# Batch 0 of a fused attention and feed-forward kernel: the first two head pairs' kv moved ahead of the second transposes

## The chip, the cores and the metric

The kernel runs on one core of one Trainium2 chip. A core has five engines that run their own instruction queues in order: TensorE (PE in the profile, its weight loads PEld), VectorE (DVE), ScalarE (ACT), GpSimd (POOL) and SyncE (SP), which here issues nearly all DMAs. TensorE writes to PSUM, which has eight banks; the other engines copy from there to SBUF. The metric is the time of one execution on the device in microseconds (us). Lower is better. The kernel before takes 256.82 us, the median of three runs (256.74 to 257.05).

## The reference

Inputs are q, k, v of shape 8 x 8 x 576 x 64 (batch, heads, sequence, head dimension) and two weights, `w_in` of 512 x 2048 and `w_out` of 2048 x 512. The first part is attention without a square matrix:

```python
q_s = exp(q - max(q, -1)); q_s = q_s / sum(q_s, -1)      # softmax over the head dimension
k_s = exp(k - max(k, 2));  k_s = k_s / sum(k_s, 2)       # softmax over the sequence
kv  = einsum('bhsd,bhse->bhde', k_s, v)
x   = einsum('bhsd,bhde->bhse', q_s, kv)                 # then heads side by side: 4608 x 512
```

The second part is a feed-forward layer on those 4608 rows: `h = x @ w_in`, `g = 0.5 * h * (1 + erf(h / sqrt(2)))`, `out = g @ w_out`.

## The kernel before, in words

The work goes batch by batch, 512 rows of each at a time (a ninth step does the 64 rows that are left of each batch). Every batch has the same stages: exp of q and k on ScalarE, sums and scaling of q on VectorE and GpSimd, transposes of the scaled q on TensorE, `kv`, then `x`, then `h` with its gelu, then `y`. From batch 1 on, the first three stages of a batch are done while TensorE is in the `h` and `y` of an earlier one. Batch 0 has nothing to hide behind: its stages stand at the start of the kernel, while q, k, v and the weights still arrive. `h` of batch 0 is the first of the long matmul stages.

The program is written with a manual schedule: on each engine the instructions stand in the order in which the Python code issues them, and semaphores make an engine wait where it needs another's result. So the order of the calls near the end of the kernel function is the order of the queues. For batch 0 the steps are these; a "half" is two of the four head pairs.

- `tp_mm(0, half)` (L287): eight 128x128 transposes of the scaled q into one PSUM bank. `tp_evac` copies the bank to `qT`; the first half is VectorE's (L296), the second ScalarE's (L298).
- `cast_v(0, hp, engine)`: v of one head pair, 128 x 576, from float32 to bfloat16 into `v_aug`. Pairs 0 and 1 are ScalarE's (L188), 2 and 3 are GpSimd's (L190). Each waits for the DMA of its pair.
- `kv_mm(0, half)` (L225): 36 matmuls on 64x64 quarters of the array, nine steps for each of two pairs and two heads. They need the exponentials of k and the two v pieces. A column of ones in `v_aug` gives the sums of k's softmax.
- `kv_norm(0, half)`: on VectorE, per pair a reciprocal (L236) and a scaling of `kv` into `kvc` (L238).
- `x_mm(0, half)` (L343): four matmuls of 512 columns on 64x64 quarters, from `kvc` and `qT`. `x_evac` copies each pair's result to its piece of `xT`, by ScalarE (L370) or VectorE (L368). `x_tile` only takes the PSUM bank.
- `cast_wi_dm` (L848, GpSimd) and `cast_wi` (L836 on GpSimd, L837 and L840 on VectorE): columns of `w_in` to bfloat16.
- `table(AF.Gelu)` (L100): ScalarE's function table is changed from exp to gelu.
- `h_phase(0, ...)` (L377, gelu L383): the first group makes two tiles of `h` at once: for piece 0 of `xT` one matmul each, then for piece 1, and so on; each matmul has 512 columns and needs that piece and the cast weights.

`psum_h`, `psum_y` and `psum_a` hand out banks in turn (banks 0 to 2, 3 and 4, and 5). Ahead of all this stand float32 matmuls on zeros (`warm`, L899), which keep TensorE busy while the first inputs land.

Of the kernel before, what the change touches and what calls it, by code (L numbers as in the profile page):

```python
# [16 lines left out]
def kernel(  # L17
# [16 lines left out]
    nc = tc.nc  # L34
    B, H, S, D = q.shape
# [6 lines left out]
    NDM = DM // 128  # L42
    NDF = DF // 128
    NS = S // 64
# [24 lines left out]
    psum_h, psum_y, psum_a = Banks(0, 1, 2), Banks(3, 4), Banks(5)  # L69
# [9 lines left out]
    v_aug = [singles.tile([128, HP, NS, VW], BF16, name=f"v_aug{i}") for i in range(2)]  # L79
# [22 lines left out]
    st = [dict() for _ in range(B + 1)]  # L102
# [78 lines left out]
                func=AF.Exp,  # L181
            )

    def cast_v(b, hp, eng=nc.vector):
        o = v_aug[b % 2][:, hp, :, 0:D]
        i = st[b]["vf"][:, hp, :].rearrange("p (n d) -> p n d", n=NS)
        if eng is nc.scalar:
            eng.copy(out=o, in_=i)  # L188
        else:
            eng.tensor_copy(out=o, in_=i)  # L190

    def cast_v_all(b):
        for hp in range(HP):
            cast_v(b, hp, nc.gpsimd)

    def kv_tiles(b, banks=(6, 7)):


        two = [bank(i, "kv", (128, 2, 256)) for i in banks]
        if b == 0:  # L200
            p = [psum_h.tile([128, 512], FP32, tag="h", name="kv")[:, 0:256] for i in range(2)]
            p += [ps[:, 0] for ps in two]
        else:
            st[b]["kvall"] = two
            p = [two[i // 2][:, i % 2] for i in place]
        st[b]["kv"] = p
# [3 lines left out]
    def kvc_of(b, hp):  # L210

        return kvc[b][:, hp if b < 2 else place[hp], :]

    def kv_mm(b, half):


        if "kv" not in st[b]:
            kv_tiles(b)
        for n in range(NS):
            for i in range(2):  # L220
                for hh in range(2):
                    hp = 2 * half + i
                    pr = slice(hh * 64, hh * 64 + 64)
                    c = slice((hh ^ i) * 64, (hh ^ i) * 64 + 64)
                    nc.tensor.matmul(  # L225
                        st[b]["kv"][hp][c, 0:D + 1], ek[b % 2][pr, hp, n, :],
                        v_aug[b % 2][pr, hp, n, 0:D + 1], start=(n == 0), stop=(n == NS - 1),
                    )

    def kv_norm(b, half=None):  # L230

        if half is not None:
            hps = (2 * half, 2 * half + 1)
            rec = small.tile([128, 2], FP32, tag="reck")
            for i, hp in enumerate(hps):
                nc.vector.reciprocal(rec[:, i:i + 1], st[b]["kv"][hp][:, D:D + 1])  # L236
            for i, hp in enumerate(hps):
                nc.vector.tensor_tensor(  # L238
                    out=kvc[b][:, hp, :], in0=st[b]["kv"][hp][:, 0:D],
                    in1=rec[:, i:i + 1].to_broadcast([128, D]), op=ALU.mult,  # L240
                )
            return
        for i, ps in enumerate(st[b]["kvall"]):
            rec = small.tile([128, 2], FP32, tag="reck")
            nc.vector.reciprocal(rec, ps[:, :, D])
            nc.vector.tensor_tensor(
                out=kvc[b][:, 2 * i:2 * i + 2], in0=ps[:, :, 0:D],
                in1=rec.unsqueeze(2).to_broadcast([128, 2, D]), op=ALU.mult,
            )
# [28 lines left out]
    def tp_mm(b, half):  # L278
        if half == 0:
            st[b]["qT"] = attn_sb.tile([128, J, HP, 128], BF16, tag="qT", name="qT", bufs=1)  # L280
        pool, tag = (psum_h, "h") if half == 1 else (psum_a, "a")
        ps = pool.tile([128, J, 2, 128], BF16, tag=tag)
        st[b][f"tp{half}"] = ps
        for i in range(2):
            hp = 2 * half + i
            for j in range(J):
                nc.tensor.transpose(  # L287
                    ps[:, j, i, :],
                    st[b]["eq"][:, j, 2 * hp:2 * hp + 2, :].rearrange("p h d -> p (h d)"),
                    identity,  # L290
                )

    def tp_evac(b, half, eng="v"):
        o = st[b]["qT"][:, :, 2 * half:2 * half + 2, :]
        if eng == "v":
            nc.vector.tensor_copy(out=o, in_=st[b][f"tp{half}"])  # L296
        else:
            nc.scalar.copy(out=o, in_=st[b][f"tp{half}"])  # L298
# [29 lines left out]
    def x_tile(b, hp, pool, tag):  # L328
        if "xT" not in st[b]:
            st[b]["xT"] = attn_sb.tile([128, HP, M], BF16, tag="xT", name="xT", bufs=1)  # L330
        st[b][f"x{hp}"] = pool.tile([128, M], FP32, tag=tag, name="ps")

    def x_mm(b, half):

        for bb in range(B if b == B else 1):
            for r in range(2):
                for i in range(2):
                    hp = 2 * half + i
                    pr = slice(r * 64, r * 64 + 64)
                    c = slice((r ^ i) * 64, (r ^ i) * 64 + 64)  # L340
                    ps = st[b][f"x{hp}"]
                    if b < B:
                        nc.tensor.matmul(  # L343
                            ps[c, :], kvc_of(b, hp)[pr], st[b]["qT"][pr, :, hp, :],
                            start=True, stop=True,
                        )
                    else:
                        nc.tensor.matmul(
                            ps[c, bb * R:(bb + 1) * R], kvc_of(bb, hp)[pr],
                            st[b]["qT"][pr, bb // 2, hp, bb % 2 * R:(bb % 2 + 1) * R],  # L350
                            start=(bb == 0), stop=True, skip_group_check=True,
                        )
# [12 lines left out]
    def x_evac(b, hp, eng="v"):  # L365
        ps = st[b][f"x{hp}"]
        if eng == "v":
            nc.vector.tensor_copy(out=st[b]["xT"][:, hp, :], in_=ps)  # L368
        else:
            nc.scalar.copy(out=st[b]["xT"][:, hp, :], in_=ps)  # L370
# [446 lines left out]
    def load_wi(i):  # L817

        w = wst.tile([128, NDM, 512], FP32, tag=f"w{i}", name="w")
        n = wi_cols[i]  # L820
        src = moe_w_in[:, wi_off[i]:wi_off[i] + n].rearrange("(c p) f -> p c f", p=128)
        d = NDM // wi_parts[i]
        for c in range(0, NDM, d):
            nc.sync.dma_start(out=w[:, c:c + d, 0:n], in_=src[:, c:c + d])
        return w
# [3 lines left out]
    def cast_wi(i, w, eng):  # L829
        n = wi_cols[i]  # L830
        r = n // 128
        o = wi_bf[:, :, wi_off[i]:wi_off[i] + n].rearrange("p d (c m) -> p d c m", c=r)
        w = w[:, :, 0:n].rearrange("p d (m c) -> p d c m", c=r)
        if eng == "pv":

            nc.gpsimd.tensor_copy(out=o[:, 0:2], in_=w[:, 0:2])  # L836
            nc.vector.tensor_copy(out=o[:, 2:4], in_=w[:, 2:4])  # L837
        else:
            for c in range(NDM):
                nc.vector.tensor_copy(out=o[:, c], in_=w[:, c])  # L840

    def cast_wi_dm(i, w, dm, eng):

        n = wi_cols[i]
        r = n // 128
        o = wi_bf[:, dm, wi_off[i]:wi_off[i] + n].rearrange("p (c m) -> p c m", c=r)
        w = w[:, dm, 0:n].rearrange("p (m c) -> p c m", c=r)
        eng.tensor_copy(out=o, in_=w)  # L848
# [63 lines left out]
    wi = [load_wi(i) for i in range(5)]  # L912
# [21 lines left out]
    norm_q(0, 1, 2, nc.vector)  # L934
    tp_mm(0, 0)
    cast_v(0, 0, nc.scalar)
    cast_v(0, 1, nc.scalar)
    tp_evac(0, 0)
    cast_v(0, 2, nc.gpsimd)
    cast_v(0, 3, nc.gpsimd)  # L940
    x_tile(0, 0, psum_y, "y")
    x_tile(0, 1, psum_y, "y")
    tp_mm(0, 1)
    tp_evac(0, 1, "s")
    x_tile(0, 2, psum_a, "a")
    kv_mm(0, 0)
    kv_norm(0, 0)
    kv_mm(0, 1)
    kv_norm(0, 1)
    for dm in range(NDM):  # L950
        cast_wi_dm(0, wi[0], dm, nc.gpsimd)
    x_tile(0, 3, psum_h, "h")
    x_mm(0, 0)
    x_evac(0, 0, "s")
    x_evac(0, 1)
    x_mm(0, 1)
    x_evac(0, 2, "s")
    x_evac(0, 3)
    cast_wi(1, wi[1], "pv")
    table(AF.Gelu)  # L960

# [190 lines left out]
```

## Time and profile before

| What | Value |
|---|---|
| median of 3 runs | 256.82 us |
| the profiled execution, time and span | 257.07 us, 255.3 us |
| TensorE busy | 248.8 us, 97% of the span |
| VectorE, ScalarE, GpSimd busy | 82%, 74%, 27% |
| first transposes start | 10.63 us |
| first `h` matmul of batch 0 starts | 14.35 us |
| `h` of batch 0, 64 matmuls | 14.35 to 28.34 us |
| mean granted clock of TensorE | 0.996 |

Times within the profile count from the start of the span. The profiled execution took 257.07 us in all, so 1.8 us lie around its span. A row of the timeline has a start, a length, the engine, the line of the kernel, the operation, what it writes and reads, how many instructions are merged, and in brackets how long the engine stood idle before it and what ended that. The matmul rows overlap, as matmuls are pipelined: the length of one is the time to its result, while the next starts much sooner.

### The profile page before, as it was taken

How to read it: one execution, taken by the hardware profiler on the slowest of the kernel's cores; microseconds unless marked ns; L12 is line 12 of the kernel's file. 1: busy time of each engine (PE TensorE's matmuls, PEld its weight loads, DVE VectorE, ACT ScalarE, POOL GpSimd, SP SyncE). 2: the span in 40 equal slices, each digit the busy share in tenths (PEclk: the TensorE clock that was granted, in tenths of full speed). 3: DMA queues.
4: the chain of work that ended last, by engine and by line, in shares of the span. 5: the costliest groups of instructions: out<-in, count | busy, mean ns of one | idle time of the engine just before them, and what ended most of it. 6: DMA issues, size and time to landing. Idle time of an engine off the chain costs nothing.

```text
span 255.3 us, 6533 instructions
## 1 busy us (share of the span) xinstructions
PE 248.8 (97%) x2678; PEld 196.1 (77%) x2678; DVE 208.1 (82%) x365; ACT 188.9 (74%) x320; POOL 67.8 (27%) x65
## 2 busy tenths in 40 slices
PE   7999999999999999999999999999999999999993
PEld 3444445448888888888888888888888888888882
DVE  1878796998986989897889788988898889488962
ACT  4875996699977995899589968896886787148720
POOL 1430034000735067006700580058001800040000
PEclk9999999999999999999999999999999999999998
DMA  7999999994449925980499059904920340022024
GB/s 236 396 389 424 403 406 399 400 410 166 62 143 335 265 65 126 328 336 1 114 299 369 7 95 314 374 3 86 270 63 3 82 164 3 0 87 82 1 54 113
DMA packets 43166, 50.23 MB, mean 197 GB/s; under 512 B 20224, under 2 KB 30464, under 8 KB 42880
## 3 DMA queue, kind: packets, MB, share of 16 engines
q1 hardware_dynamic: 42496, 49.19, 58.0%
q10 hardware_dynamic: 640, 0.62, 1.0%
q8 instruction: 21, 0.34, 0.5%
q14 instruction: 9, 0.07, 0.1%
HBM read 36.70 MB, written 9.44 MB: 181 GB/s over the span
## 4 chain that ended last, share of the span: by engine, by line
PE 93%; DMA 4%; POOL 1%; DVE 0%; issue 0%; SPq 0%
PE qa L497 19%; PE ps L377 11%; PE ya L694 10%; PE qb L497 10%; PE yd L694 10%; PE ye L694 6%; PE ps L637 5%; PE yb L694 5%; PE qc L497 5%; PE yx L694 4%; DMA f<-in_v_dram 2%; PE kv L225 2%; PE ps L343 2%; DMA f<-in_q_dram 2%; PE ya L765 1%; PE yd L765 1%
## 5 line engine op out<-in xcount | busy, mean ns | idle before, releaser
L497 PEld LDWEIGHTS <-quad_s 128*128 128x128 bf16 x448 | 43.8, 98 | 5.3 <-issue 0.2
L694 PEld LDWEIGHTS <-g 128*128 128x128 bf16 x448 | 43.3, 98 | 5.8 <-issue 0.4
L269 POOL TENSOR_TENSOR e<-e,recq 128x2048 bf16<-128x2048 bf16 (+1 forms) x9 | 27.4, 3048 | 72.5 <-DVE recq L264 47.4
L694 PEld LDWEIGHTS <-s 128*128 128x128 bf16 x336 | 32.9, 98 | 3.8
L497 PEld LDWEIGHTS <-wi_bf 128*128 128x128 bf16 x336 | 32.8, 98 | 3.9
L497 PE MATMUL qa<-quad_t,quad_s 128*128 128x256 bf16 x224 | 29.3, 272 | 0.0
L377 PE MATMUL ps<-xT,wi_bf 128*128 128x512 bf16 x128 | 28.1, 379 | 0.0
L428 POOL TENSOR_TENSOR y_sb<-y_sb 128x512 f32<-128x512 f32 x14 | 19.5, 1391 | 24.2 <-DVE y_sb L428 21.3
L263 DVE TENSOR_REDUCE qsum<-e 128x16 f32<-128x1024 bf16 (+1 forms) x12 | 20.9, 1742 | 5.0 <-ACT e L173 5.0
L377 PEld LDWEIGHTS <-wi_bf 128*128 128x128 bf16 x128 | 12.3, 97 | 15.2 <-issue 0.8
L428 DVE TENSOR_TENSOR qb<-qa,r 128x512 f32<-128x512 f32 x28 | 18.1, 693 | 5.8 <-ACT g L521 3.1
L505 ACT COPY qc<-qa 128x512 f32<-128x512 f32 x26 | 13.9, 577 | 12.0 <-PE qa L497 11.5
L383 ACT ACTIVATE g<-ps 128x512 bf16<-128x512 f32 x32 | 17.7, 602 | 6.0 <-PE ps L377 5.7
L521 ACT ACTIVATE g<-r 128x512 bf16<-128x512 f32 x28 | 17.3, 633 | 6.2 <-DVE r L428 6.2
L173 ACT ACTIVATE e<-f 128x512 bf16<-128x512 f32 (+1 forms) x42 | 20.5, 559 | 1.5 <-DMA f<-in_q_dram 1.4
L521 ACT ACTIVATE g<-qc 128x512 bf16<-128x512 f32 x28 | 15.2, 595 | 7.6 <-PE qc L497 7.6
L428 DVE TENSOR_TENSOR r<-qa,r 128x512 f32<-128x512 f32 x28 | 18.0, 685 | 0.9 <-PE qa L497 0.7
L190 POOL CAST v_aug<-f 128x576 bf16<-128x576 f32 x26 | 17.7, 713 | 3.9 <-DMA f<-in_v_dram 3.7
L402 DVE TENSOR_TENSOR s<-g 128x1024 bf16<-128x1024 bf16 x28 | 18.6, 684 | 0.0
L178 ACT ACTIVATE ek<-f 128x2304 bf16<-128x2304 f32 (+1 forms) x10 | 17.4, 1738 | 0.6 <-DMA f<-in_k_dram 0.5
L521 ACT ACTIVATE g<-qb 128x512 bf16<-128x512 f32 x28 | 15.1, 595 | 0.7 <-PE qb L497 0.7
L497 PE MATMUL qb<-quad_t,quad_s 128*128 128x256 bf16 x112 | 15.5, 273 | 0.0
(101 smaller groups left out, 468.7 us busy)
## 6 DMA issues: line engine op xcount, KB each, us to landing
out_dram<-y_sb SPq DMA_DIRECT2D x16, 512.0 KB, 3.4
f<-in_k_dram SPq DMA_DIRECT2D x6, 1152.0 KB, 10.2
f<-in_v_dram SPq DMA_DIRECT2D x6, 1152.0 KB, 11.8
f<-in_q_dram SPq DMA_DIRECT2D x6, 1024.0 KB, 8.2
w<-in_moe_w_in_dram SPq DMA_DIRECT2D x6, 512.0 KB, 8.1
f<-in_v_dram SPq DMA_DIRECT2D x8, 288.0 KB, 6.6
f<-in_q_dram SPq DMA_DIRECT2D x4, 512.0 KB, 9.0
w<-in_moe_w_out_dram SPq DMA_DIRECT2D x2, 1024.0 KB, 11.8
```

What stands on the lines that cost most here:

```text
L173: nc.scalar.activation(out=dst[:, i], in_=src[:, u], func=AF.Exp)
L178: nc.scalar.activation(out=ek[b % 2][:, i:i + n], in_=st[b]["kf"][:, i:i + n].rearrange("p x (n d) -> p x n d", n=NS), func=AF.Exp,)
L190: eng.tensor_copy(out=o, in_=i)
L263: nc.vector.reduce_sum(out=qsum, in_=st[b]["eq"][:, :, i * w:(i + 1) * w, :], axis=AX.X)
L269: eng.tensor_tensor(out=e, in0=e, in1=st[b]["recq"].unsqueeze(3).to_broadcast([128, J, w, D]), op=ALU.mult,)
L377: nc.tensor.matmul(ps, wi_bf[:, dm, t * 128:(t + 1) * 128], st[c]["xT"][:, dm, :], start=(dm == 0), stop=(dm == NDM - 1),)
L383: nc.scalar.activation(out=st[c]["g"][:, t, :], in_=ps, func=AF.Gelu)
L402: tt(out=s12[:, a, half], in0=g[:, a, half], in1=g[:, b, hi], op=ALU.add)
L428: eng.tensor_tensor(out=out, in0=in0, in1=in1, op=op)
L497: nc.tensor.matmul(held[kind, q][:, u], w, mov[m][:, k], start=(m in (1, 5) and u == 0 and k == 0), stop=(k == 1), skip_group_check=True,)
L521: nc.scalar.activation(out=g[:, t:t + 2, half], in_=held[kind, q], func=AF.Gelu)
L694: nc.tensor.matmul(ps[:, j * HN:(j + 1) * HN], act[m][:, k, j * 128:(j + 1) * 128], wgt[m][:, k, :], start=(first and k == 0 and j == 0), ...
```

## The change

Five things change, all for batch 0:

- `kv_mm(0, 0)` and `kv_norm(0, 0)` stand ahead of the second transposes `tp_mm(0, 1)`.
- `x_mm(0, 0)` stands behind these and ahead of `kv_mm(0, 1)` and `kv_norm(0, 1)`.
- The v cast of pair 3 is split: steps 0 to 4 of 9 by GpSimd, steps 5 to 8 by ScalarE. `cast_v` gets an argument `n` for that.
- The copies of x swap engines: pairs 0 and 2 by VectorE, 1 and 3 by ScalarE; before it was the other way round.
- The GpSimd casts of `w_in`'s first columns are issued earlier in the code. On GpSimd's queue they keep their place, behind the v casts.

The banks that `psum_h` hands out change with the order: the first kv half takes banks 0 and 1, the second transposes bank 2, and pair 3 of `x` bank 0. No DMA is moved, and no work is added but for one more instruction on ScalarE.

```diff
-    def cast_v(b, hp, eng=nc.vector):
-        o = v_aug[b % 2][:, hp, :, 0:D]
-        i = st[b]["vf"][:, hp, :].rearrange("p (n d) -> p n d", n=NS)
+    def cast_v(b, hp, eng=nc.vector, n=slice(0, NS)):
+        o = v_aug[b % 2][:, hp, n, 0:D]
+        i = st[b]["vf"][:, hp, :].rearrange("p (n d) -> p n d", n=NS)[:, n]
...
     cast_v(0, 1, nc.scalar)
     tp_evac(0, 0)
     cast_v(0, 2, nc.gpsimd)
-    cast_v(0, 3, nc.gpsimd)
+    cast_v(0, 3, nc.gpsimd, slice(0, 5))
+    cast_v(0, 3, nc.scalar, slice(5, NS))
+    for dm in range(NDM):
+        cast_wi_dm(0, wi[0], dm, nc.gpsimd)
     x_tile(0, 0, psum_y, "y")
     x_tile(0, 1, psum_y, "y")
+    kv_mm(0, 0)
+    kv_norm(0, 0)
     tp_mm(0, 1)
     tp_evac(0, 1, "s")
-    x_tile(0, 2, psum_a, "a")
-    kv_mm(0, 0)
-    kv_norm(0, 0)
+    x_mm(0, 0)
     kv_mm(0, 1)
     kv_norm(0, 1)
-    for dm in range(NDM):
-        cast_wi_dm(0, wi[0], dm, nc.gpsimd)
+    x_tile(0, 2, psum_a, "a")
     x_tile(0, 3, psum_h, "h")
-    x_mm(0, 0)
-    x_evac(0, 0, "s")
-    x_evac(0, 1)
+    x_evac(0, 0)
+    x_evac(0, 1, "s")
     x_mm(0, 1)
-    x_evac(0, 2, "s")
-    x_evac(0, 3)
+    x_evac(0, 2)
+    x_evac(0, 3, "s")
```

## The prediction

> **What bounds the kernel now.** I read the page first, busy times and the chain, to see which engine sets the end.
>
> ```profile
> PE 248.8 (97%) x2678; PEld 196.1 (77%) x2678; DVE 208.1 (82%) x365; ACT 188.9 (74%) x320; POOL 67.8 (27%) x65
> PE 93%; DMA 4%; POOL 1%; DVE 0%; issue 0%; SPq 0%
> ```
>
> TensorE is busy for 97% of the span and is 93% of the chain. Next the waits of TensorE alone, over the whole span:
>
> ```profile
> PE ps L899 <- DVE scr L95: 1.5, 1, 1.5
> PE kv L225 <- POOL v_aug L190: 0.5, 1, 0.5
> PE ps L343 <- DVE kvc L238: 0.3, 1, 0.3
> ```
>
> After the start it waits twice, both times in the stretch that the change rewrites. From 14.35 us on the list is empty. So what counts is when the first `h` matmul of batch 0 (L377) starts: what it loses or gains goes to the end one for one. Then the timeline of that stretch, start and length in us:
>
> ```profile
> 10.34 1.23 ACT L188 CAST v_aug<-f 128x576 bf16<-128x576 f32 x2
> 10.63 1.06 PE L287 MATMUL ps<-identity,e 128*128 128x128 bf16 x16
> 11.47 1.37 POOL L190 CAST v_aug<-f 128x576 bf16<-128x576 f32 x2 [1.63 <-DMA f<-in_v_dram]
> 11.62 0.79 PE L225 MATMUL kv<-v_aug,ek 64*64 64x65 bf16 x38
> 11.72 1.01 ACT L298 COPY qT<-ps 128x1024 bf16<-128x1024 bf16 x1 [0.15 <-PE ps L287]
> 12.34 0.36 DVE L238 TENSOR_TENSOR kvc<-kv,rec 128x64 bf16<-128x64 f32 x2
> 12.89 0.47 PE L225 MATMUL kv<-v_aug,ek 64*64 64x65 bf16 x34 [0.49 <-POOL v_aug L190]
> 13.18 0.41 PE L343 MATMUL ps<-qT,kvc 64*64 64x512 bf16 x4
> 13.40 0.23 DVE L236 RECIPROCAL rec<-kv 128x1 f32<-128x1 f32 x2 [0.69 <-PE kv L225]
> 13.60 0.35 DVE L238 TENSOR_TENSOR kvc<-kv,rec 128x64 bf16<-128x64 f32 x2
> 13.61 0.59 ACT L370 CAST xT<-ps 128x512 bf16<-128x512 f32 x1 [0.88 <-PE ps L343]
> 13.87 1.31 DVE L368 CAST xT<-ps 128x512 bf16<-128x512 f32 x2
> 13.88 0.54 PE L343 MATMUL ps<-qT,kvc 64*64 64x512 bf16 x4 [0.30 <-DVE kvc L238]
> 14.35 13.99 PE L377 MATMUL ps<-xT,wi_bf 128*128 128x512 bf16 x64
> ```
>
> See three things. The second eight transposes run while TensorE waits for the second v cast anyway (it ends at 11.57, `kv` starts at 11.62). The 0.49 us wait is for the fourth v cast on GpSimd (ends 12.84). And `xT` piece 0 is copied by ScalarE from 13.61, ready at 14.20, before TensorE gets to `h`. Single starts and ends below come from the same timeline asked in windows of some tenths of a us.
>
> **The change, part by part.**
>
> *First kv half ahead of the second transposes.* Its start is set by the v casts, not by its place: still 11.62, last matmul issued 11.90. Its two `kvc` pieces are ready at 12.57 and 12.70, as before. The eight transposes lose their cover. They now come behind it, across one more change from 64x64 pieces to the full array: 0.14 us from the last kv matmul to the next full one (41.20 to 41.35 in batch 1, and the same at five later places). So they start at 12.05, eight steps of 0.056, the last at 12.44, results at 12.65. Before: 11.69. TensorE idles some 0.45 us, from 11.17 to 11.62, in their old place.
>
> *The ScalarE copy of them* (1.01 us) starts at 12.69 and ends at 13.70 instead of 12.73. Its readers, the second half of `x`, come at 13.99 (below): covered by 0.3.
>
> *Last v piece split.* GpSimd does five ninths: 0.37 by share of its 0.666 row, at most the whole row, so from 12.17 to 12.54 or 12.84. I take 0.42, ending at 12.59, as it is nearer to the share. ScalarE does four ninths, 256 elements a row: between 0.40 (an exp of 256 elements) and 0.66 (its cast of 576); I take 0.40, the row of that size. It waits for the piece's DMA (issued 6.80, landing 5.3 us later, 12.1) and ends at 12.55, or 12.8. Behind it in ScalarE's queue stands the copy of the transposes, which can't start before 12.69: nothing, or at worst 0.14 of the 0.3 us of cover above. GpSimd's weight casts keep their place in its queue, and the first waits for its DMA until 13.60 either way: nothing. No DMA is moved; SP's queue is unchanged.
>
> *First x half ahead of the second kv half.* It follows `kvc` by 0.05, as the row at 13.88 follows the piece ready at 13.83: 12.62, and 12.76 for the second pair. In batch 1 the same four matmuls followed by a kv half take 0.53 from the last x start to the last kv start (42.97 to 43.50). So the last kv matmul starts at 13.29; before 13.18. The 0.49 us wait is gone and x with its transposes took its place: +0.11. VectorE's norm ends at 14.07 (13.96), the second x half starts at 13.99 and 14.13 (13.88 and 14.02), and TensorE could start `h` at 14.13 + 0.33 = 14.46 (0.33 is 14.02 to 14.35 now, and 45.015 to 45.348).
>
> *Copies of x swap engines.* Piece 0 is now VectorE's, and VectorE's queue has the second norm ahead of it: the copy is put behind a step that itself waits for the kv half. It starts at 13.87 + 0.11 = 13.98, takes the 0.686 of its row, ends at 14.67, and `h` starts 0.05 later at 14.72. Bounds: 14.46 if that copy didn't gate (+0.11), 14.87 if the first weight load adds its whole 0.10 and a wait step some 0.05 (+0.52). I take 14.72. Piece 1 (ScalarE, from 13.69 to 14.28), pieces 2 (VectorE to 15.29) and 3 (ScalarE to 15.16) are needed at 15.17, 15.60 and 16.03: nothing. ScalarE's table load moves from 15.06 to 15.17, so the first gelu could start at 16.57; the first `h` tile is done at about 16.4, and its bank isn't wanted again before 18: nothing. VectorE's weight cast ends at 16.07 instead of 15.96 and is read at 16.9.
>
> Sum: 14.72 - 14.35 = +0.37 us, carried to the end by a TensorE with no wait left to absorb it. The one gap below the list's threshold, 0.2 us before 44.05, is ScalarE's copy of an x that TensorE made, and moves along. The profiled execution takes 257.07 (span 255.3 and 1.8 around it), 0.25 above the median of the runs, 256.82. So 257.44 for it, and 256.82 + 0.37 = 257.19 for a median: 257.2. What a measurement of this kernel tells from no change is about 0.2%, 0.51 us; this is 0.15%.
>
> **Rivals.**
>
> *Slower by more than 0.2%: the first weight load of `h`.* Now it waits for GpSimd's cast alone, and its matmul for ScalarE. In the changed program the load itself waits for VectorE's copy and GpSimd. If the change of array shape and the load (0.098) start only then, the 0.12 us of the first (0.33 less 0.21 of streaming) and the second come on top: 14.72 + 0.22 = 14.94, +0.59, 257.4. It decides from a start of 14.86 on. For it: the wait is in the program. Against: at 13.88 a load that waits for `kvc` starts with its matmul, which takes 0.400 instead of 0.375, so 0.025 more.
> The Trainium skill, "TensorEngine Tiling (Array Packing)", section "Key Properties", says that a change of tiling mode drains the TensorE. By that rule the first load could not have run ahead before either, the drain would be over by 14.46, and this rival would shrink to its load; the trace agrees, as that load starts only at 14.345, with its matmul. The rule also counts against the change, which has two such changes more.
>
> *Less: the copy doesn't gate,* and `h` starts near 14.46: +0.11, 256.93. For it only that VectorE may get through its norm sooner; against it, VectorE's order, in which nothing can pass.
>
> *Faster: the wait that goes is not replaced.* The most to win is both waits, 0.79 us: 256.03. It would need `h` before 13.84, while the second norm alone ends no sooner than now. With just the earlier v piece, 0.25 at most: 256.6.
>
> *The clock falls.* TensorE's idle stretches grow: 0.45, then 0.7 from 13.3 to 13.99, then 0.3. At the start of the kernel the same weight loads take 0.34 us, one per 0.86, and from 7.6 on 0.19, one per 0.43: half pace exists on this trace. If the first eight `h` matmuls ran so, 8 x 0.216 = 1.73 more: 258.9. Against: idle of 0.49 and 0.30 now leaves the granted clock at 1.00 in every slice from 10 to 28 us.
> The Trainium skill, "TensorE: Matmul & The Clock Gate", section "What's actually happening", puts the fall after an idle window of some 3.4 us; by that rule 0.7 us does nothing. No run so far shows a longer gap.
>
> **How the numbers follow.** My sum (+0.25 to +0.51) 0.46; the copy not gating 0.10; the weight load, or any other 0.15 us on top, 0.33; the clock 0.06; faster 0.05. So within 0.2%: 0.46 + 0.10 = 0.56, slower 0.33 + 0.06 = 0.39, faster 0.05. The range leaves out the faster case, part of the ungated one, the clock and the tail of the slower: 256.8 to 257.75.
>
> **What would show it.** Right: no kv wait on GpSimd; transposes of the second half at 12.05, its copy from 12.7; the second kv half from 13.0; `xT` piece 0 on VectorE from 13.98; the first L377 matmul at 14.72, and behind it a wait by VectorE named in TensorE's list; then nothing until the end. Wrong: a start before 14.4 or after 14.86, a new TensorE wait later on, or a granted clock under 1.00 behind 14 us.

## The result

The changed kernel takes 257.14 us, the median of 22 runs, against 256.81 for the kernel before in the same sessions. The ratio is 1.0012, with a 95% interval of 1.0006 to 1.0017: 0.33 us slower, between 0.15 and 0.44. That is a loss, though a smaller one than 0.2%.

The two profiled spans don't show it: both are 255.3 us. The list of TensorE's waits in the changed kernel (what waited, for what, us in total, times, longest):

```profile
PE ps L899 <- DVE scr L95: 1.5, 1, 1.5
PE ps L343 <- DVE kvc L238: 0.5, 1, 0.5
PE kv L225 <- ACT v_aug L188: 0.4, 1, 0.4
PE ps L377 <- POOL wi_bf L848: 0.3, 1, 0.3
```

The wait for GpSimd's v cast is gone. Two new ones stand in its place, for the second v cast on ScalarE and ahead of the first `h` matmul, and the wait for the second norm has grown from 0.3 to 0.5 us. The timeline of the same stretch, start and length in us:

```profile
9.94 1.23 ACT L188 CAST v_aug<-f 128x576 bf16<-128x576 f32 x2
11.21 0.47 PE L225 MATMUL kv<-v_aug,ek 64*64 64x65 bf16 x34 [0.36 <-ACT v_aug L188]
11.62 0.62 PE L287 MATMUL ps<-identity,e 128*128 128x128 bf16 x8
11.74 0.41 ACT L188 CAST v_aug<-f 128x256 bf16<-128x256 f32 x1 [0.57 <-DMA f<-in_v_dram]
12.20 0.54 PE L343 MATMUL ps<-qT,kvc 64*64 64x512 bf16 x4
12.28 1.01 ACT L298 COPY qT<-ps 128x1024 bf16<-128x1024 bf16 x1
12.44 0.60 PE L225 MATMUL kv<-v_aug,ek 64*64 64x65 bf16 x36
13.30 0.36 DVE L238 TENSOR_TENSOR kvc<-kv,rec 128x64 bf16<-128x64 f32 x2
13.57 1.28 DVE L368 CAST xT<-ps 128x512 bf16<-128x512 f32 x2
13.58 0.54 PE L343 MATMUL ps<-qT,kvc 64*64 64x512 bf16 x4 [0.53 <-DVE kvc L238]
14.40 2.53 PE L377 MATMUL ps<-xT,wi_bf 128*128 128x512 bf16 x11 [0.28 <-POOL wi_bf L848]
```

The order is the forecast one: kv half, transposes, x half, kv half, x half, with `xT` piece 0 on VectorE directly behind the norm. But the whole picture stands 0.40 us further left than in the first profile: ScalarE's two v casts end at 11.17 (9.94 + 1.23) instead of 11.57 (10.34 + 1.23), as ScalarE waited less ahead of them: 0.40 us for the second piece of q instead of 0.58, and its second exponential of k started 1.05 us behind the first instead of 1.30. So times counted from the span's start can't be compared. Counted from the end of ScalarE's second v cast, `h` starts at 14.40 - 11.17 = 3.23 us, against 14.35 - 11.57 = 2.78 before. From the first `h` matmul to the end of the span it is 240.94 us in both: nothing is made up later. From here on "start of `h`" means the time behind that cast.

### The profile page after: what moved, and what is told of

It is laid out like the page before. It is cut to its first block, busy times and chain, and to the rows that moved or that the text cites. A ratio compares the mean times of both kernels' runs of the same rounds, so it can differ in the third digit from the quotient of the medians.

```text
span 255.3 us, 6535 instructions
## 1 busy us (share of the span) xinstructions
PE 248.3 (97%) x2678; PEld 196.1 (77%) x2678; DVE 208.3 (82%) x365; ACT 188.9 (74%) x321; POOL 67.5 (26%) x65
## 4 chain that ended last, share of the span: by engine, by line
PE 93%; DMA 4%; POOL 0%; ACTq 0%; issue 0%; SPq 0%; DVE 0%
PE qa L497 19%; PE ps L377 11%; PE ya L694 10%; PE qb L497 10%; PE yd L694 10%; PE ye L694 6%; PE ps L637 5%; PE qc L497 5%; PE yb L694 5%; PE yx L694 4%; DMA w<-in_moe_w_in_dram 2%; PE kv L225 2%; DMA touch<-in_moe_w_in_dram 2%; PE ps L343 2%; PE ya L765 1%; PE yd L765 1%
## 5 line engine op out<-in xcount | busy, mean ns | idle before, releaser
L190 POOL CAST v_aug<-f 128x576 bf16<-128x576 f32 (+1 forms) x26 | 17.3, 700 | 5.2 <-DMA f<-in_v_dram 5.1
```

## The experiments

| Kernel | median, us | ratio to before (95%) | start of `h`, us |
|---|---|---|---|
| before, first profile | 256.81 | | 2.78 |
| before, second profile | | | 2.95 |
| the change | 257.14 | 1.0012 (1.0006 to 1.0017) | 3.23 |
| change, copies of x given back | 256.79 | 0.9997 (0.9988 to 1.0006) | 2.88 |
| before, v split alone | 256.80 | 1.0004 (0.9995 to 1.0012) | 2.90 |
| before, copies of x swapped alone | 256.96 | 1.0005 (0.9996 to 1.0014) | 3.06 |
| change, transposes put back | 257.71 | 1.0032 (1.0022 to 1.0043) | 3.92 |
| before, first kv half ahead alone | 256.81 | 0.9999 (0.9990 to 1.0008) | 2.73 |
| copies back, second kv half ahead of x | 256.83 | 1.0001 (0.9992 to 1.0010) | 2.66 |
| the same, transposes in two banks | 256.75 | 0.9997 (0.9988 to 1.0006) | 2.57 |

Each ratio is to runs of the kernel before in the same session (medians of 256.77 to 256.81). Each start is a difference of rows of that kernel's profile. The interval of a ratio is 0.2 us to either side, so the times alone decide only the larger steps; the rest is read from the starts.

### The copies of x given back

```diff
-    x_evac(0, 0)
-    x_evac(0, 1, "s")
+    x_evac(0, 0, "s")
+    x_evac(0, 1)
     x_mm(0, 1)
-    x_evac(0, 2)
-    x_evac(0, 3, "s")
+    x_evac(0, 2, "s")
+    x_evac(0, 3)
```

> The change with the copies of x given back as before: pieces 0 and 2 to ScalarE, 1 and 3 to VectorE. Theory A: the loss is the copy of x piece 0, which stands in VectorE's queue behind the second norm. ScalarE is free for it 0.02 us after its copy of the transposes, 0.4 us ahead of VectorE, so h starts when TensorE gets to it, 0.33 us after the last x matmul. Counted from the end of ScalarE's second v cast, h starts at 2.88 us (the change: 3.23, before: 2.78): 0.35 us less than the change, some 0.1 us (0.04%) over before. Theory B: the loss is the order on TensorE (the first x half ahead of the second kv half, and two more changes of array shape). Then this kernel stays at the change's time, +0.33 us over before (1.0012).

From its timeline, ScalarE's two v casts, the copy of `xT` piece 0 and what follows on TensorE:

```profile
9.84 1.23 ACT L188 CAST v_aug<-f 128x576 bf16<-128x576 f32 x2
13.09 0.59 ACT L370 CAST xT<-ps 128x512 bf16<-128x512 f32 x1
13.48 0.54 PE L343 MATMUL ps<-qT,kvc 64*64 64x512 bf16 x4 [0.53 <-DVE kvc L238]
13.95 2.33 PE L377 MATMUL ps<-xT,wi_bf 128*128 128x512 bf16 x10
```

The copy is done at 13.68, before the second x half has run, and `h` starts without a wait, 0.47 us behind the start of that x half instead of 0.82. The start of `h` is 2.88, as expected, 0.35 less than in the change, and the time is level with before. So the loss goes with one item of the change, the engines of the copies. The edit gives all four back; that piece 0 is the one that counts is read from the trace, where `h` starts behind it. The rest of the change, taken together, costs nothing that these runs can tell.

This also settles whose wait the last line of the change's list is. It names GpSimd's weight cast, but the piece that the first load needs was cast from 13.18 to 13.59. What ended late was VectorE's copy, at 14.25; the trace has a wait step of 0.051 us on TensorE's load queue from 14.29, and the load at 14.37.

### The copies swapped alone

The kernel before with the swap of the previous diff the other way round, and nothing else.

> The kernel before with nothing but the copies of x swapped: pieces 0 and 2 on VectorE, 1 and 3 on ScalarE. Theory A: that alone makes the loss. VectorE copies piece 0 behind the second norm, from 13.87 to 14.55 in the times of before, and h's first weight load waits for it with a wait step of its own: h starts 3.13 us after ScalarE's second v cast (before: 2.78), +0.35 us (1.0014). Theory B (the order on TensorE makes the loss): no change, 1.000.

```profile
10.05 1.23 ACT L188 CAST v_aug<-f 128x576 bf16<-128x576 f32 x2
13.61 1.28 DVE L368 CAST xT<-ps 128x512 bf16<-128x512 f32 x2
14.34 1.89 PE L377 MATMUL ps<-xT,wi_bf 128*128 128x512 bf16 x8 [0.19 <-DVE xT L368]
```

Here the profile names VectorE's copy itself as what ended the wait. `h` starts at 3.06, against 2.78 and 2.95 before. The time, by its ratio 0.13 us over before with an interval from -0.10 to +0.36, is on that side without being clear of zero. Against the first profile the swap alone costs 0.28, against the second 0.11: less than the expected 0.35. There is no wait step in this program: the first weight load ran ahead, at 14.08, and the matmul alone waited for the copy (14.29) and started 0.05 behind it.

### The split of the last v cast alone

```diff
-    cast_v(0, 3, nc.gpsimd)
+    cast_v(0, 3, nc.gpsimd, slice(0, 5))
+    cast_v(0, 3, nc.scalar, slice(5, NS))
```

> The kernel before with nothing but the split of the last v cast (five ninths GpSimd, four ninths ScalarE). Theory A: the second kv half waits for this cast in the kernel before (0.49 us) and the piece is ready 0.25 us sooner, so everything behind it moves by that: h starts 2.53 us after ScalarE's second v cast (before: 2.78), the time falls by 0.25 us (0.9990). Theory B: ScalarE now stands waiting for the piece's DMA with the copy of the second transposes queued behind, so that copy ends at about 13.55 instead of 12.73, and the second x half waits for it rather than for kv: a gain of 0.1 us or none.

```profile
9.41 1.67 DVE L269 TENSOR_TENSOR e<-e,recq 128x1024 bf16<-128x1024 bf16 x1
9.85 1.23 ACT L188 CAST v_aug<-f 128x576 bf16<-128x576 f32 x2
11.22 0.61 PE L287 MATMUL ps<-identity,e 128*128 128x128 bf16 x8 [0.20 <-DVE e L269]
11.76 0.85 PE L225 MATMUL kv<-v_aug,ek 64*64 64x65 bf16 x72
12.77 1.00 PE L343 MATMUL ps<-qT,kvc 64*64 64x512 bf16 x8 [0.15 <-DVE kvc L238]
13.34 1.07 ACT L370 CAST xT<-ps 128x512 bf16<-128x512 f32 x2 [0.43 <-PE ps L343]
13.98 2.32 PE L377 MATMUL ps<-xT,wi_bf 128*128 128x512 bf16 x10 [0.21 <-ACT xT L370]
```

The wait for the fourth v cast is gone (72 kv matmuls in one run), and still nothing is won. Neither theory had the reason. The second transposes waited for VectorE's scaling of q, which ended at 11.08 (9.41 + 1.67), and the first kv half behind them started 0.68 us after the v cast, not 0.05. So its `kvc` came late, the first x half waited for it, and ScalarE's copy of piece 0 behind that. I had taken the first kv half's start for one set by v.

### The transposes put back

The change with these two lines moved back ahead of `kv_mm(0, 0)`.

```diff
+    tp_mm(0, 1)
+    tp_evac(0, 1, "s")
     kv_mm(0, 0)
     kv_norm(0, 0)
-    tp_mm(0, 1)
-    tp_evac(0, 1, "s")
     x_mm(0, 0)
```

> The change with the second transposes (and their place in the queue, not the engine of their copy) put back ahead of the first kv half; x order, split and swapped copies stay. Theory A: the late transposes cost nothing by themselves, as the first x half waits for kvc anyway: h at 3.23 us after ScalarE's second v cast, the time of the change (+0.33 us over before, 1.0012). Theory B: the two more changes of array shape (0.1 us each) and the lost cover are part of the loss: 0.15 to 0.2 us less than the change, h at about 3.05.

```profile
9.42 1.70 DVE L269 TENSOR_TENSOR e<-e,recq 128x1024 bf16<-128x1024 bf16 x1
9.85 1.23 ACT L188 CAST v_aug<-f 128x576 bf16<-128x576 f32 x2
10.56 1.30 PE L287 MATMUL ps<-identity,e 128*128 128x128 bf16 x16
11.80 0.48 PE L225 MATMUL kv<-v_aug,ek 64*64 64x65 bf16 x36
12.81 0.54 PE L343 MATMUL ps<-qT,kvc 64*64 64x512 bf16 x4 [0.53 <-DVE kvc L238]
13.05 0.60 PE L225 MATMUL kv<-v_aug,ek 64*64 64x65 bf16 x36
15.00 1.24 PE L377 MATMUL ps<-xT,wi_bf 128*128 128x512 bf16 x5 [0.28 <-DVE xT L368]
```

Both theories were wrong: it is neither level with the change nor faster, but 0.6 to 1.1 us slower than before, and its start of `h`, 3.92, is 0.69 behind the change's. The scaling ends at 11.12 (9.42 + 1.70), the second half of the transposes comes behind it, and the first kv half starts at 11.80, 0.72 behind the v cast instead of 0.04. With the x half ahead of the second kv half, that lateness has no cover: x waits for `kvc`, the second kv half for x, and all else behind. So moving the kv half ahead of the transposes, which the sum priced at nothing, is what makes the new order of x bearable.

### The kernel before, profiled again

> The kernel before once more, for a second profiled execution. Theory A: the execution profiled at first was an unusual one, in which v's casts came 0.65 us behind the scaling of q; in most executions the second transposes, which need that scaling, end later than the second v cast and hold the first kv half back. Then the first kv matmul pair stands 0.3 us or more behind the end of ScalarE's second v cast (0.05 in the first profile) and h starts 2.85 to 2.95 us behind it (2.78). Theory B: the first profile is typical: 0.05 and 2.78 again.

```profile
PE ps L287 <- DVE e L269: 0.5, 1, 0.5
PE ps L287 <- POOL e L269: 0.2, 1, 0.2
```

```profile
10.13 1.23 ACT L188 CAST v_aug<-f 128x576 bf16<-128x576 f32 x2
11.55 0.61 PE L287 MATMUL ps<-identity,e 128*128 128x128 bf16 x8 [0.55 <-DVE e L269]
12.09 1.07 PE L225 MATMUL kv<-v_aug,ek 64*64 64x65 bf16 x72
14.31 1.89 PE L377 MATMUL ps<-xT,wi_bf 128*128 128x512 bf16 x8
```

Same program, other waits: the two of the first profile are gone, and the second transposes wait 0.5 us for the scaling of q. The first kv half starts 0.73 behind the v cast (0.05 in the first profile), `h` at 2.95. So the first profile caught an execution in which v's casts came late against q: they ended 0.65 us behind the scaling of q, in the other 13 profiles between 0.06 ahead of it and 0.39 behind. All five further profiles of kernels with the transposes first (this one, the split alone, the swap alone, the transposes put back, and the one with less of `w_in` below) have kv 0.29 to 0.73 behind the cast. Counted from VectorE's scaling, all five agree: kv starts 0.68 us behind its end, and 0.15 behind the start of the last transpose.

The first profile itself has this limit too. Its kv started 0.15 us behind the last transpose (11.47), and TensorE's list has no wait for v there: the transposes, which came right behind the matmuls on zeros, were done just as v was. So TensorE did not wait for the second v cast, as the prediction reads the rows at 11.57 and 11.62; two limits fell together, and one of them was taken for the cause.

### The first kv half ahead, alone

```diff
+    kv_mm(0, 0)
+    kv_norm(0, 0)
     tp_mm(0, 1)
     tp_evac(0, 1, "s")
     x_tile(0, 2, psum_a, "a")
-    kv_mm(0, 0)
-    kv_norm(0, 0)
     kv_mm(0, 1)
```

> The kernel before with one thing of the change: the first kv half and its norm ahead of the second transposes. Theory A (late q scaling in most executions): the first kv half starts 0.05 us after ScalarE's second v cast, the second still waits for GpSimd's whole v cast (1.33), x follows at 1.6, and h starts at 2.75 to 2.80: 0.1 us under before. Theory B (my sum): the first half was never held back, the transposes only lose their cover: h not sooner than in before.

```profile
10.03 1.67 DVE L269 TENSOR_TENSOR e<-e,recq 128x1024 bf16<-128x1024 bf16 x1
10.47 1.23 ACT L188 CAST v_aug<-f 128x576 bf16<-128x576 f32 x2
11.75 0.47 PE L225 MATMUL kv<-v_aug,ek 64*64 64x65 bf16 x34 [0.30 <-ACT v_aug L188]
14.43 1.90 PE L377 MATMUL ps<-xT,wi_bf 128*128 128x512 bf16 x8
```

The kv half starts 0.05 behind the v cast, though the scaling of q ended only at 11.70 in this execution (with the transposes first it would have come 0.68 behind that, by the five profiles above), and `h` starts at 2.73: less than in either profile of before, by 0.05 and 0.22. The time is level (0.9999). It supports theory A in the trace; a gain in time of 0.1 us is below what eleven runs show.

### Two steps further

The kernel with the copies given back, and the first x half behind the second kv half again:

```diff
     tp_evac(0, 1, "s")
-    x_mm(0, 0)
     kv_mm(0, 1)
     kv_norm(0, 1)
+    x_mm(0, 0)
```

> The change with the copies of x given back as before, and the first x half put behind the second kv half again. Kept: first kv half ahead of the second transposes, split v cast. Theory A: kv's second half then needs only its v pieces and the transposes, starts 1.06 us after ScalarE's second v cast instead of 1.28 and ends 0.25 us sooner; h starts at 2.65 to 2.70, held by ScalarE's copy of x piece 0 behind its copy of the transposes. That is 0.55 us under the change and 0.2 us (0.1%) under before. Theory B: the order of x and kv is worth nothing, h at 2.89 as with the copies given back alone, the time that of before.

Then the same with the second transposes in two banks:

```diff
-    tp_evac(0, 1, "s")
+    nc.scalar.copy(out=st[0]["qT"][:, :, 2, :], in_=st[0]["tp1"][0])
+    nc.vector.tensor_copy(out=st[0]["qT"][:, :, 3, :], in_=st[0]["tp1"][1])
```

> As the kernel with the second kv half ahead of the first x half, and the second transposes go to two banks, one copied by ScalarE, one by VectorE between its two norms. Theory A: ScalarE is then free for x piece 0 by 1.75 us after its second v cast, x piece 0 is copied by 2.45, and TensorE itself (2.60) sets the start of h: 0.3 us (0.1%) under before. Theory B: GpSimd's cast of the first weight columns, which waits for its DMA and ends 2.44 behind that cast, or VectorE's norm behind the extra copy, holds h at 2.65 or later: no gain over the kernel without this step.

Both starts came as expected, 2.66 and 2.57. Both times are level with before (256.83 and 256.75 against 256.77), where the starts, against 2.78 and 2.95, say 0.1 to 0.3 and 0.2 to 0.4 us less. The profile of the first has no reason for it: from the first `h` matmul to the end it took 240.91 us, as in before. The profile of the second has one, in the waits from 13 to 30 us:

```profile
DVE wi_bf L844 <- DMA w<-in_moe_w_in_dram: 2.4, 3, 1.5
PEld L381 <- DVE wi_bf L844: 1.1, 3, 0.5
```

(Lines 844 and 381 are 840 and 377 of the kernel before.) VectorE waited for the DMAs of `w_in`, and TensorE's weight loads for VectorE's casts, inside `h`. From the first `h` matmul to the end this execution took 241.40 us instead of 240.94: 0.46 us given back.

### With a quarter of w_in left out

To see whether the arrival of `w_in` takes the gains back in general, four kernels without the load of its fourth block:

```diff
-    wi = [load_wi(i) for i in range(5)]
+    wi = [load_wi(i) for i in (0, 1, 2, 4)]
+    wi.insert(3, wi[2])
```

> The kernel before, with the fourth block of w_in (512 of 2048 columns, 1 MB) left out: it isn't loaded, the third block's values are cast in its place, so a quarter of h is made from other weights. All else stays, the casts too. It is the base line for the three runs beside it. Theory A (in part of the executions the last blocks of w_in arrive just in time, and h can't run earlier than they do): the kernel before starts h late enough, and this saves it 0.1 us at most (0.9996 to 1.000). Theory B (arrival doesn't matter): the same.

> The kernel with the copies of x given back and the second kv half ahead of the first x half, with the fourth block of w_in left out in the same way. Theory A: with the weights no longer late, the earlier start of h (2.67 us after ScalarE's second v cast, against 2.78 to 2.95 before) reaches the end: 0.2 us or more under the base line without that block, where with the block it was level with before. Theory B: the arrival of w_in isn't what took the gain; level with the base line again.

> The change, with the fourth block of w_in left out in the same way. Theory A: its h starts 3.23 us after ScalarE's second v cast in any case and late weights don't bind it; the loss to the base line is what the start of h says, 0.3 to 0.45 us (1.0012 to 1.0018). Theory B: the same, so this run doesn't tell the two apart; it tells whether the loss of the change depends on the weights at all. If it vanished, the loss would be one of the weights' arrival.

> The kernel with the second transposes in two banks, with the fourth block of w_in left out in the same way. Theory A: h starts 2.58 us after ScalarE's second v cast and no later wait takes it back (0.47 us of its 0.37 us gain and more were taken back by waits for the last blocks in the profiled execution with the block): 0.3 us under the base line. Theory B: level with the base line.

| Kernel without that block | median, us | ratio to the full kernel before (256.74) |
|---|---|---|
| before (base line) | 256.90 | 1.0006 (0.9997 to 1.0014) |
| copies back, second kv half ahead of x | 256.62 | 0.9995 (0.9986 to 1.0003) |
| the change | 257.28 | 1.0023 (1.0014 to 1.0032) |
| two banks | 256.73 | 0.9994 (0.9985 to 1.0003) |

The change loses 0.38 us to its base line, as with all weights: its loss doesn't hang on the arrival of this block. The other two are 0.28 and 0.17 below the base line, on the side of theory A, but the intervals overlap. Their profiles have the expected starts of `h`: 2.88 in the base line, then in the order of the table 2.66, 3.24 and 2.59. From the first `h` matmul to the end of the last one it is 236.75 us in the first three and 236.87 in the last, so even without that block 0.12 us are given back there. That late weights eat the gain is shown for one execution and not for the medians; it stays open. No kernel here beats before by more than the measurement tells.

## Why the prediction was right

It said 257.2, with a range of 256.8 to 257.75 and a loss within 0.2% as the likeliest case; 257.14 was measured. Step by step, on the clock of the second v cast:

- **The x half in the place of the wait (+0.11)**: right. The second x half was forecast 2.42 behind the cast (13.99 - 11.57) and came at 2.41 (13.58 - 11.17).
- **Piece 0 behind the norm on VectorE (from 14.46 to 14.72)**: right in place, and the largest term. Its copy was forecast at 2.41 and started at 2.40. Giving it back to ScalarE took 0.35 us off the start of `h`; the sum had 0.26, and the next point the rest.
- **`h` 0.05 behind that copy**: too little. It was 0.15 (14.25 to 14.40). The rival of the first weight load was partly true: the wait step and the load cost 0.10 more, of the 0.22 that it would have added.
- **Nothing absorbs it**: right, 240.94 us from `h` to the end in both.
- **The late transposes and the split cost nothing**: right. ScalarE's copy of the transposes ended at 13.29, 0.29 ahead of its reader at 13.58.
- **The first kv half isn't moved, "its start is set by the v casts, not by its place"**: wrong in five of the six profiles of kernels with the transposes first, and the step that failed. In the one profile that I had the place set the start as much as v did: the transposes and the cast allowed kv at the same moment, so moving it gained nothing there. In the second, the transposes held the kv half back by 0.68 us, and the change does remove that. The gain is small in the kernel before, whose fourth v cast covers most of it (`h` at 2.95 instead of 2.78).

So two errors met. Against the first profile the change costs 3.23 - 2.78 = 0.45, more than the forecast 0.37, for the weight load; against the second it costs 0.28. The measured 0.33 lies between them. The size came out right in part by luck, because one miss made up for the other. The clock stayed at full pace behind the longer gaps (granted clock 1.00 from 10 to 28 us), and the faster case did not come.

## What to carry to other kernels

A copy that swaps engines takes the place of the new engine's queue: look at what stands ahead of it there, and whether that itself waits for the engine that needs the copy. Where several input streams set the start of a kernel, one profile shows one order of arrival; a wait that is absent from it can be the rule, and a start that follows one event closely may follow a second one just as closely. So compare two profiles of the same program, and count times from an event common to both, not from the start of the span. A stage that is moved ahead of another may be worth nothing in the old order and a lot in the new one.

## What the runs showed of the hardware

VectorE's scaling of q's second half takes 1.27 us in one execution and 1.72 in another, on the same data sizes. The rows of GpSimd's scaling of the first half and of VectorE's, in the kernel with the copies of x given back:

```profile
8.14 1.90 POOL L269 TENSOR_TENSOR e<-e,recq 128x1024 bf16<-128x1024 bf16 x1 [6.83 <-DVE recq L264]
9.40 1.72 DVE L269 TENSOR_TENSOR e<-e,recq 128x1024 bf16<-128x1024 bf16 x1
```

GpSimd ends at 10.04, VectorE at 11.12, 1.08 later. In the first profile it was 9.83 and 10.91, again 1.08, with a row of 1.27 that had started 0.19 before GpSimd's end. In all 14 profiles the difference is 1.08 us, while the time that the two rows overlap goes from 0.19 to 0.64: VectorE makes no progress on this scaling, which reads two operands from SBUF, as long as GpSimd runs its own. So the second transposes hang on GpSimd's first half, and with it on when the first piece of q lands: in all 14 profiles VectorE's scaling ends 5.92 us, to 0.01, behind the start of the first exponential of q. That is how the order of arrival decides the wait. The Trainium skill, "SBUF — State Buffer", section "SBUF: two separate sides", says that the two engines share a pair of ports that the one who starts first holds for its whole instruction while the other fully blocks; the trace agrees, with these 1.08 us.

The half pace of TensorE at the start ended at 7.6 us in the first profile (weight loads of 0.34, then 0.19) and at 5.8 in the change's, so the matmuls on zeros were over at 10.79 and 9.82 by their rows. In the first profile the transposes stood right behind them, and kv behind these. Even so it cost `h` nothing: kv, at 11.62, could not have started sooner, as v's cast ended at 11.57.
